# First step's values in place, dense weights in seven pieces, late values of two groups in whole tiles, own places for the first and last steps

## Chip, cores, metric

One core of a Trainium2 chip. The metric is the device time of one execution in microseconds (us), lower is better. The kernel before: median 1637.58 us of 3 runs (1636.99 to 1638.34). PE is TensorE, DVE VectorE, ACT ScalarE, POOL GpSimd, SP SyncE, whose queue issues most transfers.

## The reference

A recurrent attention layer (32 heads of 128, segments of 32 tokens, 8 memory rows carried from segment to segment) and a dense layer (512 to 1376 to 512), each applied twice to 2048 tokens:

```python
mem = mem0
for s in range(64):
    h = concat([mem, x[:, 32*s:32*s+32]])              # 40 rows
    q, k, v = h @ Wq, h @ Wk, h @ Wv                   # 32 heads
    o = softmax(mask(q @ k.T * scale)) @ v  @ Wo
    mem = o[:, :8]; outs.append(o[:, 8:])
# x += A(ln(x)); x += relu(ln(x) @ w1) @ w2; and both once more
```

Segment s+1 needs the memory rows of segment s: 64 steps in a row, four more because the second layer runs four steps behind the first.

## The kernel before

A planner written in Python holds every operation with a cost, an engine (or a choice of two) and a priority (`PLACE`, `AHEAD`: fitted numbers), simulates the engines, and emits the instructions in the order of the simulated starts. Each engine then works through its list strictly in that order. Cuts are marked `[...]`.

```python
# values of a step's own rows: product into vw, then small copies into V0
def step_values(k):
    [...]
    if 1 in act: values(...)                     # both layers
    else:        values_narrow(HTs[i][...])      # one layer: four strips
    place_values(k, False)                       # four DMAs V0 <- vw, step 0's on ACT's queue

# dense weights, once "loaded" holds (step 1's values are placed)
def load_dense():
    def dma1(): nc.sync.dma_start(out=w1_sb[:], in_=B_w1...)                 # 1376 KB
    def dma2(): nc.sync.dma_start(out=w2_sb[:, 0:NFC - 1, :], in_=B_w2...)   # 1280 KB
                [...]                                                         # and the rest, 96 rows

# values of the memory-independent rows of groups 6..15 ("late"), one group at a time,
# in tiles of 64 rows; layernorm two steps ahead of the first product
def late_values(g, xnT, ps, gate=()): [...]

o.prio = PERIOD * o.step + PLACE.get((o.key, o.step % 2), 0.0)   # same places for all steps
```

## Time and profile before

How to read it: the prediction below shows the page's busy shares, the table of stages, the starved stretch in step 1 and the loads of step 0. Of the rest of the page these two lines matter: how many packets the transfers make, and that one queue carries instructions.

```profile
DMA packets 35486, 64.30 MB, mean 39 GB/s; under 512 B 7224, under 2 KB 19232, under 8 KB 35104
q8 instruction: 318, 5.21, 1.3%
```

318 packets and 5.21 MB are 16 KB each: one block of 256 PE instructions per packet (PE and its weight loads have 81170 instructions, 317 blocks).

The stages used below are: step 0 (the weights stream in), steps 1, 2 and 3, the 60 wide steps (both layers at work), steps 64 to 66, and the last step with the tail. There is one trace of this kernel. Its execution took 1634.85 us, 2.7 us less than the median of the timed runs.

### The profile page before, as it was taken

Reading aid. Unit: us, or ns where it says so; the run is one execution under the profiler, and the core shown is the slowest. Engines: PE = TensorE matmul, PEld = TensorE weight load, DVE = VectorE, ACT = ScalarE, POOL = GpSimd, SP = SyncE. Lnnn points to the kernel's source line nnn. Section 1 sums busy time; section 2 is a strip of 40 time slices with the busy share of each in tenths; the row PEclk is TensorE's granted clock in tenths of the full one; section 3 lists DMA queues with packets and bytes.
Section 4 is the critical chain, followed back from the end, with each engine's and each line's share of the span. In section 5 each row is a group of like instructions: output and inputs, shape, how many; then the busy total and the mean of one; then the engine's idle time right before and its main releaser. Section 6 shows DMA issues by size and latency. Waiting matters only on the chain.

```text
span 1632.9 us, 89617 instructions
## 1 busy us (share of the span) xinstructions
PE 1592.1 (97%) x40555; PEld 1372.8 (84%) x40615; DVE 1124.5 (69%) x3113; ACT 1047.2 (64%) x2625; POOL 147.0 (9%) x354
## 2 busy tenths in 40 slices
PE   6899999999999999999999999999999999999998
PEld 4788888888888888888888888888888888888886
DVE  4476776776776676677677677667677766766765
ACT  4566666676666666666666666666666666666654
POOL 3110000010100000000000010010000000000010
PEclk9999999999999999999999999999999999999999
DMA  9711001110100110010010110011010000000000
GB/s 357 259 31 31 23 24 29 29 34 18 39 18 28 28 30 25 25 37 21 26 29 24 31 32 24 18 35 26 25 38 21 24 24 25 18 19 19 18 5 7
DMA packets 35486, 64.30 MB, mean 39 GB/s; under 512 B 7224, under 2 KB 19232, under 8 KB 35104
## 3 DMA queue, kind: packets, MB, share of 16 engines
q1 hardware_dynamic: 29216, 39.09, 8.6%
q0 software_dynamic: 4704, 18.35, 3.0%
q8 instruction: 318, 5.21, 1.3%
q10 hardware_dynamic: 1184, 1.12, 0.2%
q14 instruction: 64, 0.52, 0.1%
HBM read 33.50 MB, written 11.93 MB: 28 GB/s over the span
## 4 chain that ended last, share of the span: by engine, by line
PE 94%; DMA 2%; DVE 2%; ACT 1%; issue 1%; POOL 0%; POOLq 0%; DVEq 0%; ACTq 0%
PE work L907 37%; PE st L1046 19%; PE fill L827 16%; PE fill L527 10%; PE work L1019 4%; PE work L936 4%; PE work L527 2%; DMA Wk_sb<-in_A_Wk_dram 2%; ACT OT L763 1%; DVE HT L1062 0%; PE fill L636 0%; PE fill L846 0%; ACT PT L1000 0%; ACT es L958 0%; DMA V<-vw 0%
## 5 line engine op out<-in xcount | busy, mean ns | idle before, releaser
L907 PE MATMUL work<-HT,Wq_sb 128*128 128x80 bf16 (+1 forms) x8704 | 368.5, 200 | 8.4 <-DVE HT L1062 7.3
L907 PE MATMUL work<-HT,Wk_sb 128*128 128x80 bf16 (+1 forms) x8704 | 361.9, 200 | 3.7 <-DMA Wk_sb<-in_A_Wk_dram 2.5
L907 PEld LDWEIGHTS <-Wq_sb 128*128 128x128 bf16 x8704 | 325.7, 100 | 29.5 <-issue 14.8
L907 PEld LDWEIGHTS <-Wk_sb 128*128 128x128 bf16 x8704 | 326.3, 100 | 25.7 <-issue 13.6
L1046 PE MATMUL st<-OT,Wo_sb 128*128 128x80 bf16 (+1 forms) x8704 | 340.3, 200 | 3.3 <-issue 2.2
L1046 PEld LDWEIGHTS <-Wo_sb 128*128 128x128 bf16 x8704 | 320.2, 100 | 8.6 <-issue 4.9
L763 ACT CAST kT<-work 128x320 bf16<-128x320 f32 (+1 forms) x512 | 209.6, 409 | 99.1 <-PE work L907 59.2
L763 ACT CAST qT<-work 128x320 bf16<-128x320 f32 (+1 forms) x508 | 208.6, 411 | 89.9 <-PE work L907 43.9
L827 PE MATMUL fill<-Wv_sb,HT 128*64 128x512 bf16 x2048 | 259.1, 380 | 0.0
L1000 ACT ACTIVATE PT<-work,half 128x320 bf16<-128x320 f32 (+2 forms) x431 | 189.1, 466 | 56.2 <-PE work L527 35.5
L947 DVE TENSOR_TENSOR es<-work,maskb 128x320 f32<-128x320 f32 (+2 forms) x340 | 134.3, 403 | 111.6 <-PE work L936 93.9
L763 ACT CAST OT<-work 128x320 bf16<-128x320 f32 (+1 forms) x377 | 150.4, 415 | 63.5 <-PE work L1019 63.1
L763 ACT CAST vw<-fill 128x512 bf16<-128x512 f32 x204 | 119.4, 585 | 88.0 <-PE fill L827 80.1
L958 ACT ACTIVATE es<-es 128x320 f32<-128x320 f32 (+2 forms) x340 | 138.4, 409 | 42.8 <-DVE es L954 41.1
L954 DVE TENSOR_TENSOR es<-es,mx 128x320 f32<-128x320 f32 (+2 forms) x340 | 146.2, 439 | 4.5
L827 PEld LDWEIGHTS <-HT 128*64 128x64 bf16 x2048 | 98.5, 110 | 58.7
L951 DVE TENSOR_REDUCE mx<-es 128x8 f32<-128x320 f32 (+2 forms) x340 | 132.1, 398 | 4.4
L977 DVE TENSOR_TENSOR P<-es,sm 128x320 bf16<-128x320 f32 (+2 forms) x337 | 131.5, 406 | 3.4
L961 DVE TENSOR_REDUCE sm<-es 128x8 f32<-128x320 f32 (+2 forms) x340 | 131.3, 394 | 2.3 <-ACT es L958 2.0
L1002 DVE TENSOR_SCALAR PT<-work,half 128x320 bf16<-128x320 f32 (+2 forms) x249 | 109.3, 446 | 28.6 <-PE work L527 27.4
L936 PEld LDWEIGHTS <-qT 128*40 128x40 bf16 x4096 | 87.1, 98 | 44.3 <-issue 1.0
L1062 DVE CAST HT<-st 128x64 bf16<-128x64 f32 (+1 forms) x67 | 14.8, 221 | 157.8 <-PE st L1046 157.7
(91 smaller groups left out, 1807.9 us busy)
## 6 DMA issues: line engine op xcount, KB each, us to landing
V<-vw SPq DMA_DIRECT2D x252, 48.0 KB
V<-vh SPq DMA_DIRECT2D x120, 64.0 KB
vh<-vg SPq DMA_DIRECT2D x20, 256.0 KB
Wq_sb<-in_A_Wq_dram POOLq DMA_DIRECT2D x2, 2048.0 KB, 23.0
Wk_sb<-in_A_Wk_dram POOLq DMA_DIRECT2D x2, 2048.0 KB, 29.1
Wo_sb<-in_A_Wo_dram POOLq DMA_DIRECT2D x2, 2048.0 KB, 40.0
Wv_sb<-in_A_Wv_dram POOLq DMA_DIRECT2D x1, 2048.0 KB, 11.9
vh<-w_sb POOLq DMA_DIRECT2D x4, 512.0 KB, 10.6
```

Of the source, the lines that this page charges most:

```text
L527: nc.tensor.matmul(out_[u:v, :], lhsT=lhsT[:, u:v], rhs=rhs, start=start, stop=stop, tile_position=(0, u))
L763: nc.scalar.copy(out=out_, in_=in_)
L827: nc.tensor.matmul(vp[64 * b:64 * b + 64, :], lhsT=cols(c4), rhs=Wv_sb[:, c4, n * 512:(n + 1) * 512], start=(c4 == 0), stop=(c4 == NC4 - 1 ...
L907: nc.tensor.matmul(qp[:, hi * 2 * L:hi * 2 * L + n], lhsT=W_sb[:, c4, h * Dh:(h + 1) * Dh], rhs=HT[:, c4, c0:c1], start=(c4 == 0), stop=(c ...
L936: nc.tensor.matmul(v[64 * g2:64 * g2 + L, a, i, b, :], lhsT=qT[:, hi, a * L:(a + 1) * L], rhs=kT[:, hi, a * L:(a + 1) * L], start=True, st ...
L947: nc.vector.tensor_tensor(out=flat(es[:, A]), in0=flat(sp[:, A]), op=ALU.add, in1=maskb[:, a_lo:a_hi, :].unsqueeze(2).to_broadcast([128, n ...
L951: nc.vector.tensor_reduce(out=mx[:, As], in_=es3(), axis=AX.X, op=ALU.max)
L954: nc.vector.tensor_tensor(out=es3(), in0=es3(), op=ALU.subtract, in1=mx[:, As].unsqueeze(2).to_broadcast([128, ns * na, L]))
L958: nc.scalar.activation(out=es[:, A], in_=es[:, A], func=ACTF.Exp, scale=SCALE)
L977: (nc.gpsimd if eng == POOL else nc.vector).tensor_tensor(out=o, in0=flat(es[:, A]), op=ALU.mult, in1=sm[:, As].rearrange("p (a s) -> p a ...
L1000: nc.scalar.activation(out=o, in_=i, func=ACTF.Copy, scale=half[:, b:b + 1])
L1046: nc.tensor.matmul(wo[:, 2 * W * c4 + c0:2 * W * c4 + c1], lhsT=Wo_sb[:, h, c4 * 128:(c4 + 1) * 128], rhs=OT[:, h, c0:c1], start=(h == 0 a ...
```

## The change

Intent: a shorter step 0; no burst of dense weights that starves PE of instructions; fewer PE instructions for the late values; and priorities fitted for the first and last steps alone. The core of the diff (the tables of fitted numbers and the plumbing are cut):

```diff
-            o.prio = PERIOD * o.step + PLACE.get((o.key, o.step % 2), 0.0)
+            o.prio = PERIOD * o.step + PLACE.get((o.key, phase(o.step)), 0.0)
+def phase(step):
+    return 2 + (step > 0) + (step == 2) if step < DELTA else step % 2 + 5 * (step >= STEPS)
 [...]
+        if k == 0:
+            values_direct(HTs[0][:, :, 0:L], deps)      # products of 40 rows, evicted into V0
+            return
 [...]
-        for i, t, dma in ((0, 0.5, dma1), (1, 1.0, dma2)):
-            bulk(SP, t, dma, ("w", i), 1.4, r=["loaded", ...], w=[...])
+        def piece(at, fn, cost=0.5):                    # w1: 4 pieces, w2: 3
+            if at == (k, u):
+                bulk(SP, cost, fn, ("w", i), 0.35, r=["loaded", ("sc", k, u), ...], w=[("w", i)])
+        # at = (1,0) (1,1) (1,2) (1,3) | (1,4) (2,0) (2,1): scores of step k, unit u
 [...]
-    ahead, due = {}, {}                                 # one group at a time, first layernorm for step 4
+    start = {g: DELTA + 10 * i for i, g in enumerate(pairs)}    # pairs (6,7), (8,9), ...
+            if k == start[g] - 2:                       # first pair: layernorms in step 2
+                one = prepare_group(g, [("att", k - 1)])
+                late[g] = one, prepare_group(g + 1, [("att", k - 1)], one)
```

The lists `r=[...]` say what the planner places an operation behind.

## The prediction

> **What bounds the kernel now.** I read the page first: who is busy, and when.
>
> ```profile
> PE 1592.1 (97%) x40555; PEld 1372.8 (84%) x40615; DVE 1124.5 (69%) x3113; ACT 1047.2 (64%) x2625; POOL 147.0 (9%) x354
> ...
> PE   6899999999999999999999999999999999999998
> ...
> DMA  9711001110100110010010110011010000000000
> ```
>
> TensorE (PE) is full in every slice but the first two and the last; the DMA engines are full only in the first two slices (some 60 us, 40.8 us a slice) and nearly idle afterwards. So the end is set by PE, and what is not PE lies at the start and the end. The kernel is 68 dependent steps (a segment of 32 tokens each; two layers run four steps apart, so steps 0 to 3 and 64 to 67 hold one layer and the 60 between both). A step ends when VectorE copies the new memory rows (the evictions HT<-st, 67 of them). Cutting the trace at those gives: step 0, 1, 2, 3, the 60 wide steps, steps 64 to 66, the last with the tail.
>
> ```profile
> 0.00:55.08 55.08, 41.40 (x707) 26.38 (x707) 23.87 (x80) 26.39 (x59) 18.11 (x42) 0.97 0.99 359
> 55.08:73.92 18.84, 15.74 (x486) 13.78 (x486) 8.38 (x39) 9.87 (x35) 0.90 (x2) 0.93 0.72 251
> 73.92:92.83 18.91, 18.15 (x591) 15.73 (x591) 12.96 (x48) 10.76 (x38) 2.96 (x7) 0.98 0.21 52
> 92.83:108.70 15.87, 14.98 (x490) 13.14 (x490) 9.57 (x41) 10.20 (x36) 1.32 (x6) 1.00 0.13 29
> 108.70:1549.30 1440.60, 1427.35 (x36069) 1240.57 (x36127) 1021.70 (x2719) 945.33 (x2310) 118.26 (x286) 1.00 0.10 26
> 1549.30:1603.40 54.10, 52.96 (x1637) 45.14 (x1641) 35.11 (x139) 32.95 (x108) 4.22 (x10) 1.00 0.02 5
> 1603.40:1632.90 29.50, 21.49 (x577) 18.07 (x577) 12.94 (x49) 11.73 (x39) 1.24 (x3) 0.91 0.03 8
> ```
>
> (Columns: length, busy PE, weight loads, DVE, ACT, POOL, granted clock, DMA share, GB/s.) Of 40.8 us without PE, 13.7 are in step 0, 3.1 in step 1, 8.0 in the last window, and 13.3 in all 60 wide steps. The granted clock dips in step 1 and in the tail.
>
> The hole in step 1, in the timeline of PE:
>
> ```profile
> 68.16 0.74 PE L1046 MATMUL st<-OT,Wo_sb 128*128 128x40 bf16 x23
> 71.06 0.38 PE L1046 MATMUL st<-OT,Wo_sb 128*128 128x40 bf16 x9 [2.16 <-issue]
> 71.29 0.20 PE L527 MATMUL work<-ident,P 128*128 128x80 bf16 x1
> 71.32 0.29 PE L1019 MATMUL work<-PT,V 128*128 128x80 bf16 x2
> 71.41 1.27 PE L1046 MATMUL st<-OT,Wo_sb 128*128 128x40 bf16 x32
> ```
>
> A run of 32 projections stops after 23 and waits for no data ("issue"). Behind it 32 take 1.27 us where 0.97 is usual. In the records, full clock ends at 71.36 us and half clock lasts 3.41 us. Counting PE's instructions up to the hole and up to a smaller one (0.36 us at 76.1 us, also "issue"): 2241 and 2497, exactly 256 apart. The DMA queue marked "instruction" carries 16 KB packets, one per some 256 PE instructions; around the hole they start at 57.82, 61.33, then only 68.41 (ends 69.49, PE goes on 1.57 later), while the other queue moves 330 to 410 GB/s, mostly in 1 KB packets: the two dense weights, 1376 KB and 1280 KB in one transfer each, with five stores of activations. PE was starved of instructions by the dense loads.
>
> **What the skill says.** "Runtime: NRT & Kernel Launch", Instruction fetch mechanics: instructions are streamed in blocks of 16 KiB, 256 instructions, over DMA, normally hidden. The trace agrees on the size and shows one case where it was not hidden. "TensorE: Matmul & The Clock Gate", Part 1: idleness drops the PE clock to half, and the observing window is 3413 ns. The trace agrees: three half-clock stretches of 3.41 us, at 30.4, 71.4 and 1624.4 us, each after a gap of 2.5, 2.2 and 3.3 us. "DMA: Bandwidth & Descriptors", Queues, rings and completion order: each DMA engine takes turns between its queues packet by packet, so a bulk transfer delays others without owning them; the delayed fetch agrees. "TensorEngine Tiling (Array Packing)", Key Properties: changing the tiling mode drains TensorE; here it costs 97 ns from start to start (80-column matmul to scores 131 against 36).
>
> **The change, part by part.** I compared both instruction orders. The matmul streams are the same but for 623 fewer instructions (40615 to 39992), mostly pairs of half-width tiles becoming whole tiles. A pair of half tiles runs concurrently, so that is no PE time by itself.
>
> *Late values of two groups in whole tiles.* Before: 10 groups x 32 matmuls of 64 rows, two at a time: 320/2 x 216 ns = 34.6 us. After: 5 pairs x 32 matmuls of 128 rows: 160 x 216 = 34.6 us. Nothing gained. Mode changes: 375 before, 377 after, +0.2 us. Their stores go from 20 of 256 KB to 40 of 128 KB on a queue that has time. One buffer holds the pair, so five of the layernorm transposes that filled a step boundary move inside a step: bare boundaries (last projection straight to next Q or K) go from 27 to 31. Each boundary costs 520 ns against 36, and a transpose filled 0.22 of it: about +0.6 us.
>
> *First step in place.* Before, step 0's values took 32 matmuls in four strips (1.7 us), went to a buffer, and six DMAs on ScalarE's queue placed them (four of 48 KB, two of 64 KB). After: 32 in two strips (3.5 us), evicted straight to their place. PE work +1.7 us, but step 0 is bound by the weight stream: the last Wo half lands at 53.2 us (issue 11.0 + 42.2) and its 64 projections start at 53.27.
>
> ```profile
> Wo_sb<-in_A_Wo_dram POOLq DMA_DIRECT2D x2, 2048.0 KB, 40.0
> ...
> V<-vw ACTq DMA_DIRECT2D x4, 48.0 KB
> ```
>
> The six small DMAs ran from 17.8 to 30 us; there the rate falls from 405 to 254 GB/s, and Wk's first half comes late:
>
> ```profile
> 25.82 1.90 PE L827 MATMUL fill<-Wv_sb,xg 128*64 128x512 bf16 x16
> 30.18 1.01 PE L907 MATMUL work<-HT,Wk_sb 128*128 128x40 bf16 x27 [2.47 <-DMA Wk_sb<-in_A_Wk_dram]
> ```
>
> Without them 0.32 MB less is moved (0.8 us at 400 GB/s), and the engines that lagged stay level; I take 2 us off the last weight's landing, so step 0 ends at 53.1 instead of 55.08. The 2.5 us gap and its half clock mostly vanish, but inside a step bound elsewhere: not counted twice. **-2.0 us.**
>
> *Dense weights in seven pieces.* Each of 256 to 512 KB, released by the scores of successive units of steps 1 and 2, so the queue is never full for 4 us on end. Gone: 2.16 + 0.36 us of starvation and half of 3.41 us of half clock (1.7). **-4.2 us**, on PE's path.
>
> *Own places for first and last steps.* Only the planner's priorities. For the 60 wide steps, adding up start-to-start times (80 columns 35.9 ns, 40 columns 25.2, 128 columns 55.7, 512 columns 216 per tile set, 97 per mode change, 520 at a boundary) gives 1413.8 us before and 1412.8 after: the same. The measured 1440.6 leaves 27; the same sum misses some 0.26 us in steps where I see no wait, so true waits are about 11 us. They sit in odd steps: 22.08 us without a late-values operation, 22.48 with one, 23.02 with two (0.87 us of work each), so part of each fills a hole. After has 5, 10 and 15 such steps, before 4, 12 and 14: no difference to speak of. From better places I take **-1.5 us** here, and **-0.7** in steps 64 to 67 (65 measures 18.9 against a sum of 17.0); the final chain (turn, layernorm, dense, store) has the same operations.
>
> Sum: -2.0 - 4.2 + 0.8 - 1.5 - 0.7 = -7.6: 1637.58 to 1630.0 us.
>
> **Rivals.** (1) *The hole moves instead of vanishing*: the activations' stores (five of 128 KB, 1 KB packets) and the first pair's load still share steps 1 and 2 with the pieces, and 40-column steps use up 256 instructions in some 3.2 us, so another fetch may be late. For it: a block must arrive within about 0.75 of a block. Against: the 18 MB of weights and stores through the software queue before 59 us stopped no fetch. Time: 1634. (2) *Step 0 gains nothing*: after Wk's second half the new order has 11.5 us of PE work, before 10.5; if PE rather than Wo is last, 1632. (3) *New transfers hurt*: the late groups' activation stores become 1024 pieces of 128 bytes each, on the queue that also places values each step; a late placement would stall attention ten times by a microsecond: +5 to 10. Against: placements have over 10 us from their source to their use. (4) *Steady state improves much*: if the search removed the whole 11 us: 1621.
>
> **Range and chances.** The parts I can point at are worth 6 us; the places lie between -11 and +4. Range 1623 to 1637. Over 2% faster means below 1605, 33 us: more than all of step 0's and the tail's waits together, 0.02. Slower by 2% would need a new wait of half a microsecond in each step: 0.01. Within 2%: 0.97.
>
> **What would show it.** Right: no "issue" gap over 1 us between 55 and 95 us and full clock there; step 1 near 15.5 us; first memory eviction near 53; no DMA to V on ScalarE's queue; wide steps summing to 1436 to 1442; the tail still 29 us. Wrong: a starved gap elsewhere, first eviction at 55 or later, or two-step periods other than 47.4 to 48.4 us.

## The result, and the profile after

| | median | range | runs |
|---|---|---|---|
| before | 1637.28 us | 1636.60 to 1638.34 | 4 |
| changed | 1636.09 us | 1633.76 to 1636.44 | 4 |

Ratio 0.9989, 95% interval 0.9972 to 1.0006: the same. (Ratios are the mean time of one kernel's fast runs over that of the other's of the same rounds, so not quite the ratio of the medians.) The 7.6 us that I forecast are not there; later the changed kernel came out at ratios of 1.0002 and 1.0002. Its 15 runs have a mean of 1636.13 us, the 44 runs of the kernel before 1635.82.

The page after (busy PE, packets, the instruction queue):

```profile
PE 1589.6 (97%) x39898; PEld 1377.3 (84%) x39992; DVE 1111.6 (68%) x3091; ACT 1052.5 (64%) x2655; POOL 140.1 (9%) x352
DMA packets 47097, 63.89 MB, mean 39 GB/s; under 512 B 17784, under 2 KB 33440, under 8 KB 46720
q8 instruction: 313, 5.13, 1.4%
```

Instructions fell as intended (five blocks fewer), packets under 512 B went up by 10560, mostly the stores of late activations (ten of 1024 pieces). The table of stages, cut at the same evictions as before (length, busy PE, weight loads, DVE, ACT, POOL, clock, DMA share, GB/s):

```profile
0.00:52.65 52.65, 41.39 (x713) 26.81 (x713) 25.39 (x82) 28.10 (x61) 18.49 (x43) 1.00 0.98 369
52.65:70.62 17.97, 16.37 (x486) 13.55 (x486) 9.05 (x41) 9.96 (x35) 0.90 (x2) 0.91 0.61 206
70.62:89.86 19.24, 17.98 (x597) 15.92 (x599) 12.51 (x49) 11.56 (x40) 4.09 (x9) 1.00 0.43 116
89.86:106.84 16.98, 16.35 (x497) 13.48 (x497) 11.56 (x43) 11.37 (x39) 1.61 (x5) 1.00 0.25 48
106.84:1548.71 1441.87, 1423.17 (x35411) 1243.70 (x35503) 1005.50 (x2691) 945.56 (x2330) 111.10 (x283) 1.00 0.11 26
1548.71:1602.28 53.57, 52.85 (x1616) 45.50 (x1619) 34.84 (x138) 33.91 (x111) 3.12 (x8) 1.00 0.02 5
1602.28:1632.00 29.72, 21.45 (x582) 18.32 (x582) 12.72 (x49) 12.06 (x40) 0.79 (x2) 0.91 0.03 7
```

Step 0 is 2.43 us shorter, as forecast. Steps 1 and 2 should have given 4.2 us and gave 0.5; step 3 is 1.1 longer, and the wide steps 1.3. In step 2, PE stops again for nothing that is named (timeline of PE: start, length, what; in brackets the idle time before it):

```profile
83.56 0.19 PE L1214 MATMUL st<-OT,Wo_sb 128*128 128x40 bf16 x1
84.55 0.95 PE L1214 MATMUL st<-OT,Wo_sb 128*128 128x40 bf16 x31 [0.80 <-issue]
```

It stops after one projection of 32. This profiled run was the fastest of the four (1633.76). A second profile, of the same program, shows the same place at its worse, and what it does to step 2 (its line of the stage table; the clock is the seventh entry, 0.85):

```profile
83.94 0.19 PE L1214 MATMUL st<-OT,Wo_sb 128*128 128x40 bf16 x1
87.25 1.21 PE L1214 MATMUL st<-OT,Wo_sb 128*128 128x40 bf16 x31 [3.12 <-issue]
...
70.86:94.37 23.51, 19.84 (x597) 17.51 (x599) 12.52 (x50) 11.57 (x40) 4.09 (x9) 0.85 0.35 95
```

Counting PE's instructions from the start, the hole stands at 12.75 blocks of 256. The holes of the kernel before stood at 8.75 and 9.75 (2241 and 2497 instructions). In the second profile the packet with the next block starts at 84.8 us, when PE has already stopped; the blocks around it start their packets when PE is at 11.14 and 13.14. So the starvation was not removed. It moved to another boundary.

Why are the pieces not spread? The queue of SP (when it was busy with which issue):

```profile
62.24 1.81 SPq L514 DMA_DIRECT2D w_sb<-in_B_w_dram  x4
...
64.58 1.39 SPq L803 DMA_DIRECT2D xe<-in_A_x_dram  x1
...
66.49 1.39 SPq L811 DMA_DIRECT2D xh<-xg  x3
```

All four pieces of w1 go out in 1.81 us. In the plan each stands behind its unit's scores *and* behind "loaded" (the values of step 1 placed). But these are marks of the planner: they fix the place in SP's list, and the emitting loop then only calls the operations in that order. In none of the 18 traces does a transfer `w_sb<-in_B_w_dram` wait for a semaphore that PE raises; nearly all wait for earlier transfers alone, a few for VectorE as well. So no score releases a piece at run time. The four stand side by side in the list, behind the four copies into V, whose issues end at 61.6 us, and go out one after the other. The queue then moves 311 to 388 GB/s from 64 to 69 us. The last two w2 pieces go out together at 79.4 us, with 1024 packets of 128 bytes ahead of them, and move 341 and 329 GB/s from 82 to 84, just when block 12 is due (82.1 to 84.8 in the two profiles).

The table shows a second thing. `xe` is the input of the first late group. It stands behind the four pieces, and VectorE needs it (timeline of DVE, then of PE):

```profile
69.79 0.69 DVE L684 BATCH_NORM_STATS2 ln<-xe 128x6 f32<-128x512 bf16 x1 [1.14 <-DMA xe<-in_A_x_dram]
...
70.62 0.16 DVE L1230 CAST HT<-st 128x32 bf16<-128x32 f32 x1
```

```profile
70.83 0.34 PE L1074 MATMUL work<-HT,Wk_sb 128*128 128x40 bf16 x7 [0.84 <-DVE HT L1230]
```

The line after `xe` is the copy of the new memory rows, which starts the next step. VectorE keeps its order, so the late layernorm's wait for a transfer becomes PE's wait between steps 1 and 2. In the kernel before, the first such layernorm was at 107 us, after the dense weights.

### The profile page after: what moved, and what is told of

It reads as the page before. It is cut to its first block, busy times and chain, and to the rows that moved or that the text cites. A ratio compares the mean times of both kernels' runs of the same rounds, so it can differ in the third digit from the quotient of the medians.

```text
span 1632.0 us, 88442 instructions
## 1 busy us (share of the span) xinstructions
PE 1589.6 (97%) x39898; PEld 1377.3 (84%) x39992; DVE 1111.6 (68%) x3091; ACT 1052.5 (64%) x2655; POOL 140.1 (9%) x352
## 4 chain that ended last, share of the span: by engine, by line
PE 92%; DMA 3%; DVE 2%; ACT 2%; issue 1%; POOL 0%; ACTq 0%; SPq 0%; POOLq 0%; DVEq 0%
PE work L1074 37%; PE st L1214 18%; PE fill L973 14%; PE fill L646 10%; PE work L1187 4%; PE work L1103 4%; DMA Wo_sb<-in_A_Wo_dram 2%; PE work L646 2%; PE fill L944 2%; ACT OT L894 1%; DVE HT L1230 0%; PE fill L992 0%; DMA vw<-in_A_x_dram 0%; ACT es L1125 0%; ACT PT L1168 0%
## 5 line engine op out<-in xcount | busy, mean ns | idle before, releaser
L1074 PE MATMUL work<-HT,Wk_sb 128*128 128x80 bf16 (+1 forms) x8704 | 355.7, 199 | 9.6 <-DVE HT L1230 8.8
L1074 PE MATMUL work<-HT,Wq_sb 128*128 128x80 bf16 (+1 forms) x8704 | 349.3, 199 | 1.3 <-DVE HT L1230 0.9
L1214 PEld LDWEIGHTS <-Wo_sb 128*128 128x128 bf16 x8704 | 324.9, 99 | 28.0 <-issue 5.2
L1074 PEld LDWEIGHTS <-Wq_sb 128*128 128x128 bf16 x8704 | 320.4, 99 | 26.4 <-issue 15.1
L894 ACT CAST qT<-work 128x320 bf16<-128x320 f32 (+1 forms) x534 | 219.5, 412 | 76.8 <-PE work L1074 32.4
L973 PE MATMUL fill<-Wv_sb,HT 128*64 128x512 bf16 x2048 | 265.9, 381 | 0.0
L894 ACT CAST OT<-work 128x320 bf16<-128x320 f32 (+1 forms) x404 | 158.1, 417 | 119.8 <-PE work L1187 117.3
L1168 ACT ACTIVATE PT<-work,half 128x320 bf16<-128x320 f32 (+2 forms) x384 | 170.9, 468 | 67.1 <-PE work L646 47.0
L1114 DVE TENSOR_TENSOR es<-work,maskb 128x320 f32<-128x320 f32 (+2 forms) x340 | 136.8, 404 | 45.2 <-PE work L1103 40.3
L1170 DVE TENSOR_SCALAR PT<-work,half 128x160 bf16<-128x160 f32 (+2 forms) x296 | 127.5, 454 | 25.1 <-PE work L646 23.4
L1121 DVE TENSOR_TENSOR es<-es,mx 128x320 f32<-128x320 f32 (+2 forms) x340 | 136.7, 405 | 5.5
L1103 PEld LDWEIGHTS <-qT 128*40 128x40 bf16 x4096 | 90.8, 98 | 44.8 <-ACT kT L894 10.2
```

What stands on the lines that cost most here:

```text
L894: nc.scalar.copy(out=out_, in_=in_)
L973: nc.tensor.matmul(vp[64 * b:64 * b + 64, :], lhsT=cols(c4), rhs=Wv_sb[:, c4, n * 512:(n + 1) * 512], start=(c4 == 0), stop=(c4 == NC4 - 1 ...
L1074: nc.tensor.matmul(qp[:, hi * 2 * L:hi * 2 * L + n], lhsT=W_sb[:, c4, h * Dh:(h + 1) * Dh], rhs=HT[:, c4, c0:c1], start=(c4 == 0), stop=(c ...
L1103: nc.tensor.matmul(v[64 * g2:64 * g2 + L, a, i, b, :], lhsT=qT[:, hi, a * L:(a + 1) * L], rhs=kT[:, hi, a * L:(a + 1) * L], start=True, st ...
L1114: nc.vector.tensor_tensor(out=flat(es[:, A]), in0=flat(sp[:, A]), op=ALU.add, in1=maskb[:, a_lo:a_hi, :].unsqueeze(2).to_broadcast([128, n ...
L1121: nc.vector.tensor_tensor(out=es3(), in0=es3(), op=ALU.subtract, in1=mx[:, As].unsqueeze(2).to_broadcast([128, ns * na, L]))
```

## The experiments

All outputs are right. The kernel before ran in the same rounds; its medians were 1636.68 (first four runs), 1635.44 (next four), 1635.61 and 1635.61. The times alone settle little: executions of one and the same kernel spread over 5 us. So I split steps 1 and 2, where the kernels differ most, into three parts for every trace: holes over 0.3 us at a count of n.75 blocks ("boundary"), half of PE's busy time in half-clock stretches ("half clock", an estimate), and the rest. Each row has one trace; e6, e12, e13 and e17 are in the text alone.

| kernel | median us (range) | ratio (95%) | step 0 | steps 1+2 | boundary | half clock | rest |
|---|---|---|---|---|---|---|---|
| before | | | 55.08 | 37.75 | 2.5 | 1.6 | 33.7 |
| changed, first profile | 1636.09 | 0.9989 | 52.65 | 37.21 | 0.8 | 1.7 | 34.7 |
| e1 changed again | 1636.66 (1635.94-1638.35) | 1.0002 (0.9990-1.0015) | 52.16 | 42.20 | 4.4 | 4.6 | 33.1 |
| e16 changed again | 1635.19 (1633.28-1638.65) | 1.0002 (0.9990-1.0013) | 52.31 | 40.26 | 2.6 | 3.4 | 34.2 |
| e2 before + pieces | 1636.40 (1636.16-1636.73) | 0.9998 (0.9986-1.0011) | 55.83 | 38.54 | 2.4 | 3.1 | 33.1 |
| e3 changed, whole loads | 1636.61 (1635.59-1637.77) | 1.0000 (0.9987-1.0012) | 52.09 | 41.39 | 2.1 | 3.4 | 35.9 |
| e4 idle products | 1635.96 (1633.45-1636.76) | 0.9992 (0.9979-1.0006) | 53.43 | 41.06 | 2.0 | 2.9 | 36.2 |
| e5 stores later | 1635.17 (1631.73-1637.19) | 0.9997 (0.9985-1.0009) | 52.37 | 39.95 | 3.7 | 1.7 | 34.6 |
| e8 pieces spread | 1634.36 (1633.61-1635.57) | 0.9995 (0.9983-1.0006) | 52.46 | 39.04 | 2.5 | 1.7 | 34.9 |
| e10 values by copy | 1640.36 (1636.77-1643.31) | 1.0031 (1.0019-1.0043) | 58.13 | 37.94 | 0.5 | 1.7 | 35.7 |
| e11 input early | 1634.19 (1633.31-1638.74) | 0.9999 (0.9987-1.0012) | 52.94 | 39.33 | 2.9 | 3.0 | 33.4 |
| e14 e11 + spread | 1634.72 (1632.93-1637.59) | 0.9997 (0.9985-1.0010) | 53.89 | 40.07 | 3.5 | 1.7 | 34.8 |
| e15 all early | 1637.06 (1633.84-1638.39) | 1.0010 (0.9998-1.0023) | 53.13 | 36.61 | 1.1 | 0.0 | 35.5 |
| e18 changed + 128 instr. | 1640.12 (1638.38-1642.58) | 1.0031 (1.0019-1.0043) | 55.84 | 41.40 | 4.1 | 4.7 | 32.7 |

### Is the result what it seems? (e1, e16)

No edit: the changed kernel again.

> The changed kernel once more, unaltered, for a second profile and a tighter interval. Theory A (the windows in which the PE clock is granted run free of the kernel): steps without a clock change repeat to 0.1 us (wide steps 1441.9 us in all), while the half-clock stretch at 53.2 us may fall elsewhere or be absent, so steps 0 to 3 may differ from 106.84 us by up to 1.7 us either way. Theory B (the stretch is tied to the wait for Wo): it stands again within 0.5 us of 53.2. Time against the kernel before: 0.9985 to 0.9995, so -0.8 to -2.5 us.

> The changed kernel again, unedited, beside the candidates on the same chip. Expected 1635.5 to 1636.7; its profile shows again holes at boundaries n.75 of 256 instructions of between 2 and 5 us in steps 1 and 2 together, and the sum of steps 0 to 3 somewhere between 106.8 and 111.3 us.

Ratios 1.0002 both. Steps 1 and 2 took 42.2 and 40.3 us, so the first profile (37.2) was a lucky one. The wide steps took 1441.87, 1440.91 and 1440.73 us: they repeat to about 1 us, not to the 0.1 us that I expected. Theory B is refuted: the half clock of 53.2 us stands at 55.6 in e1, and e16 has none before 73.1. Half clock explains part of the spread: of the 15 executions, the one with a mean granted clock of 0.998 took 1633.28 us, five with 0.997 averaged 1635.50, six with 0.996 1636.51, three with 0.995 1637.39. A thousandth of 1634 us is 3.3 us at half clock, about one window of 3.41 us; one more such window costs some 1.2 us (an estimate: a straight line through the 15, which leaves more than half of their variance unexplained).

### The pieces alone, and the rest without them (e2, e3)

```diff
 # e2: the kernel before, with
-            load_dense()                      # two whole transfers
+            load_dense(k, u)                  # seven pieces, as in the change
 # e3: the changed kernel, with
-            load_dense(k, u)
+            load_dense()                      # two whole transfers in step 1
```

> The kernel before with the dense weights in seven pieces and nothing else: the orders of PE, ACT and DVE are identical, only 14 lines of the DMA queue's order differ. Theory A (the hole at 68.9 us is instruction starvation by the two large loads): the 2.16 us and 0.36 us holes and the half clock at 71.4 us go, step 1 falls from 18.84 to about 15.5 and step 2 from 18.91 to about 18.2, the whole by 4 us (1633.2). Rival (the stores of the activations starve it as well): a hole of 0.5 to 1.5 us stays somewhere in steps 1 to 2, gain 1 to 2.5 us. Rival 2 (the hole has another cause): same hole, no gain.

> The changed kernel with the dense weights loaded in two transfers as before; PE, ACT and DVE orders identical. Theory A: a hole of about 2 us marked issue comes back in step 1 or 2, about two thirds into an instruction block, with a half-clock stretch after it: +3 to +4 us against the changed kernel (1639 to 1640). Rival (the new order of the first steps alone avoids the starvation, the pieces are worth nothing): within 0.5 us of the changed kernel.

The instruction orders of PE, ACT and DVE are those of the parent kernel in both, so only transfers differ. With pieces, the kernel before loses its hole at 8.75 and gets one of 2.05 us at 12.76; boundary losses are 2.4 us against 2.5. Without pieces, the changed kernel has 0.54 us at 8.76, 0.40 at 12.75 and 1.14 at 5.75. Times: the same. The pieces move the starvation; they are worth nothing measurable.

### Keeping the clock up (e4)

```diff
+                for _ in range(22 if k == 0 and p == 2 else 0):     # while PE waits for Wo
+                    nc.tensor.matmul(wo[:, 384:512], lhsT=ident, rhs=ident, start=False, stop=False)
```

> The changed kernel with 22 idle matmuls (ident by ident, 128 columns, 55.7 ns each, 1.2 us) into unused columns of the projection bank while PE waits for the last Wo half. Theory A (that wait[...] halves the clock from 53.2 to 56.6 us): no half clock between 12 and 1620 us, step 0 unchanged at 52.6 +- 0.3, step 1 17.97 to about 16.3, whole -1.7 us. Rival (the half clock comes from the steps' low use of the array in general): a stretch appears in another window of steps 1 to 3, gain below 0.5 us.

The half-clock stretch at 53 us is gone, but so it is in e11, e14, e15 and e16 without such products: that they removed it is not shown. PE did not wait for Wo in this execution, so the products came on top, and step 0 ends at 53.43 us, not at 52.6 as expected. A stretch of 6.8 us comes at 72.9, after a wait for the late input, here at its longest (DVE, then PE):

```profile
72.94 0.69 DVE L685 BATCH_NORM_STATS2 ln<-xe 128x6 f32<-128x512 bf16 x1 [4.03 <-DMA xe<-in_A_x_dram]
...
73.77 0.16 DVE L1234 CAST HT<-st 128x32 bf16<-128x32 f32 x1
```

```profile
73.99 0.71 PE L1075 MATMUL work<-HT,Wk_sb 128*128 128x40 bf16 x16 [3.73 <-DVE HT L1234]
```

This trace is what made the second cause plain: PE waits 3.73 us for a copy that takes 0.16 us and whose engine stood waiting for `xe`.

### Which transfer starves block 12? (e5, e8, e15)

```diff
 # e5: the late pair's 128-byte stores from step 2 to step 5
+            elif g <= EARLY + 2: held.append(put_op)
 # e8: e5, and each piece is planned behind a different later operation of PE
+GATE = (scores 1.2, attention 1.0, projection 1.2, projection 1.4,
+        queries/keys 2.0, scores 2.1, scores 2.2)
 # e15: e8, input of the late pair loaded in step 0, and the last pieces earlier
+GATE = (scores 1.2, attention 1.0, projection 1.1, projection 1.2,
+        projection 1.4, queries/keys 2.0, queries/keys 2.0)
```

> The changed kernel with one thing moved: the two stores of the first late pair's activations (1024 pieces of 128 bytes each) go from step 2 to step 5; only four lines of the SyncE order differ. Theory A, the small stores delay the fetch of the instruction block that ends in step 2: no hole of 0.4 to 3.1 us at the boundary 12.75 in the trace, step 2 is 18.0 to 18.8 us (19.2 to 23.5 in the runs so far), and the median falls to about 1635. Theory B, the weight pieces beside them do it (or a fetch slow by itself): the hole stays, step 2 is 19 us or longer, the median is 1636 to 1637.

> As the run before, and the seven dense pieces are really spread: each waits for a later piece of TensorE work (scores of step 1, attention of step 1, two output projections of step 1, queries and keys of step 2, scores of step 2 twice), so that no two pieces are issued together. The orders on PE, ACT and POOL are unchanged. Theory A, starvation comes of a queue that is full for 4 us: from 64 to 86 us no 4 us have over 250 GB/s, PE has no hole over 0.4 us at a block boundary from 55 us on, steps 1 to 3 sum to 51.5 to 52.5 us (54.2 in the trace of the changed kernel, 56 to 59 in later ones), and the median is 1633 to 1634.5. Theory B, the fetch is late for another reason (any transfer, or the fetches of the other engines): holes of 0.5 us or more stay, steps 1 to 3 sum to 54 us or more, the median is 1636 to 1637.

> Candidate to beat both: the orders of PE, ACT and POOL as in the changed kernel, first late input loaded in step 0, the 128-byte stores in step 5, and all seven dense pieces issued before step 2's value placements (the last two some 6 us earlier than in the run before), so that nothing large moves when instruction block 12 is to be fetched. Theory, the hole at 12.75 is the backlog of the last two pieces: it falls to 0.5 us or less (0.4 with whole early transfers, 1.2 to 3.1 where pieces were issued at 79 to 82 us); steps 1 and 2 take 34 to 36 us; median 1632 to 1634. Rival, the short instructions of the dense layer outrun the fetch whatever moves: the hole stays at 1 us or more, median 1634.5 to 1636.

e5 refutes the small stores: they are gone and the hole at 12.75 is 2.58 us. e8 was my mistake in part: its last pieces still went out together (SP's queue; then PE's hole at 12.75):

```profile
79.56 1.35 SPq L520 DMA_DIRECT2D w_sb<-in_B_w_dram  x2
80.96 0.45 SPq L522 DMA_DIRECT2D w_sb<-in_B_w_dram  x1
```

```profile
86.34 0.82 PE L1215 MATMUL st<-OT,Wo_sb 128*128 128x40 bf16 x26 [1.22 <-issue]
```

The four copies into V0 of step 2 keep SP's queue busy from 76.0 to 79.5, and what was to be spread piled up behind them. (VectorE's order is not quite that of the changed kernel in e8, e14 and e15; those of PE, ACT and POOL are.) In e15 all pieces are issued by 73.1 us. Then the hole at 12.75 is gone (block 12's packet starts when PE is at 11.90), and there is one at 10.76, where the pieces now move:

```profile
76.05 0.25 PE L1104 MATMUL work<-kT,qT 128*40 128x40 bf16 x6
77.37 0.30 PE L1104 MATMUL work<-kT,qT 128*40 128x40 bf16 x10 [1.07 <-issue]
```

So the backlog of weights makes the large hole, and it falls on the block that is due while they move. This rests on single traces, but the difference is clear: in the twelve traces in which the last two pieces are issued together, 78 to 87 us from the start, with the places and the counts of the two kernels, the hole at 12.75 is 0.5 to 3.1 us. Steps 1 and 2 took 36.61 us without any half clock, the best of all traces. But that profile was the fastest of five executions (1633.84 us), and the median is 1637.06: no gain. What the slower four did is not in a trace.

### Is it instruction fetch? (e18, e17)

```diff
+                for _ in range(64 if k == 0 and heads[0] == 8 and W_sb is Wq_sb else 0):
+                    nc.tensor.matmul(qp[:, 384:388], lhsT=ident, rhs=ident[:, 0:4], start=False, stop=False)
```

128 more instructions in step 0, nothing else (e18); the same on top of e15 (e17).

> The changed kernel with the same 64 idle products in step 0 and nothing else. Theory, instruction fetch: the holes keep standing at a count of n.75 blocks of 256 instructions, now counted with the 128 added ones, so in front of other products than before (not ahead of the third output projection of step 2). Rival, the hole is a wait of that projection for something that the profile does not name: it stays with the projection, at a count of n.25.

> The first run of this call with 64 idle products of 4 columns added to TensorE in step 0 (128 instructions with their weight loads), which moves every block boundary by half a block in the program. If the short instructions of the dense layer make the hole of block 12, the boundary now lies 128 instructions earlier in the work and the hole changes by half a us or more; if the backlog alone makes it, nothing changes but the 0 to 1.5 us that the products cost in step 0. Median 1632.5 to 1635.

In e18 the holes stand at 9.76 and 13.75 blocks, counted with the added instructions. In the changed kernel PE stopped after the first of a unit's 32 products. In e18 that product has the count 13.25; PE passes it without a stop and stops 128 instructions later, ahead of the last product of the next unit (the second pair of lines; the first pair is the other hole, in step 1):

```profile
71.50 0.51 PE L1218 MATMUL st<-OT,Wo_sb 128*128 128x40 bf16 x14
74.39 0.61 PE L1218 MATMUL st<-OT,Wo_sb 128*128 128x40 bf16 x18 [2.38 <-issue]
...
89.81 0.94 PE L1218 MATMUL st<-OT,Wo_sb 128*128 128x40 bf16 x31
92.42 0.19 PE L1218 MATMUL st<-OT,Wo_sb 128*128 128x40 bf16 x1 [1.68 <-issue]
```

A wait for data would have stayed with its product. It is the count that decides. Step 0 is 3.5 us longer in e18, not 0 to 1.5 (55.84 us; 56.56 in e17). Of this 1.9 us are two holes at 4.75 and 5.75 blocks (0.53 and 1.35 us), which now fall into step 0 and are late fetches again; the rest is the time of the products. So e18's 1640.12 us and e17's 1638.66 (1635.84 to 1639.52, ratio 1.0015, 1.0003 to 1.0027) are mostly that price. In e17 the holes of steps 1 and 2 are small (0.71 us at 12.76, 0.41 at 13.76), but the first ends at 86.6 us, and from 82 us on the DMA moves 60 GB/s or less. In e3 there are 0.40 us at 12.75, at 88 us, though its weights had moved by 79. So small holes come without a backlog at that moment; whether the short instructions outrun the fetch there, the rival of e15, stays open.

### The late input (e11, e14, e12, e13)

```diff
 # e11: the first late input is loaded one step earlier, its layernorm stays where it was
-                one = prepare_group(g, [("att", k - 1)])
+                one = prepare_group(g, [("att", k - 1 - (k == 2))])
 # e14: e11, e5 and spread pieces
 # e12: all late pairs two steps later;  e13: e12 and spread pieces
-    start = {g: DELTA + 10 * i ...}
+    start = {g: DELTA + 2 + 10 * i ...}
```

> The changed kernel with the load of the first late pair's input issued in step 0 rather than in step 1 behind the dense pieces; the orders of PE, ACT, DVE and POOL are those of the changed kernel. Theory, a new wait made by the change: the first late layernorm now stands in VectorE's order before the memory columns of step 2, and its input lands behind the dense weights. Then VectorE's wait for that input (0.6 to 4.0 us in the five traces so far) is gone before the columns of step 2, TensorE waits under 0.4 us between steps 1 and 2 (0.8 to 3.7), and the median falls by 0.5 to 1.5 us against the changed kernel of the same call's level, to 1634.5 to 1636. Rival, the wait only shows where something else is late: TensorE still waits 0.8 us or more there for another cause, median as before.

> The candidate to beat both kernels: early load of the first late input, dense pieces spread (as in the run before), the 128-byte stores of the first late pair in step 5. PE, ACT and POOL order as in the changed kernel. By the three causes found: steps 1 and 2 without boundary holes after step 0 and without the wait for the late input take 34.5 to 36 us (37.2 to 42.2 in the changed kernel), of it 1.2 us the hole of block 5.75 that the weights make; median 1632.5 to 1634. If half-clock stretches fall there whatever is done, 1.7 us more: 1634.5 to 1635.5.

> The changed kernel with all late pairs two steps later (first late layernorms in step 4, where no dense weights move). Orders change in many steps. Same theory: no wait for the late input between steps 1 and 2, steps 0 to 3 sum to 107 to 109 us; but the planned order has steps 2, 4 and 5 longer by 2.1, 0.6 and 0.3 us than that of the changed kernel and steps 3 and 6 on shorter by 0.9 and some more, so the median is 1635 to 1637. If the wide steps lose their fitted order as they did without own places: 1640 or more.

> The run before with the seven dense pieces spread, the last two now by queries and keys and by attention of step 2. Theory, holes at instruction-block boundaries come of a full queue: the hole at boundary 12.75 (1.2 us in the first spread kernel, 0.4 to 3.1 elsewhere) is under 0.5 us; steps 0 to 3 are 1 to 2 us shorter than in the run before; median 1634 to 1635. Rival, spread or not is the same: within 0.5 us of the run before.

In e11 the orders of PE, ACT, DVE and POOL are untouched, and VectorE now comes to the copy early and waits for PE:

```profile
67.79 0.68 DVE L684 BATCH_NORM_STATS2 ln<-xe 128x6 f32<-128x512 bf16 x1
...
69.25 0.19 DVE L1230 CAST HT<-st 128x32 bf16<-128x32 f32 x1 [0.56 <-PE st L1214]
```

PE waits under 0.3 us there. Step 1 takes 16.31 us (17.97, 18.70 and 18.24 in the changed kernel), but the half clock or the hole at 5.75 that those traces have in step 1 were absent too, so this is not the wait's worth alone. That the wait was real and that the change made it is shown. But the hole at 12.75 took 2.87 us, a half-clock stretch of 6.8 us followed, and the median is 1634.19, ratio 0.9999: one cause of three removed does not show in the time. e14 removes this one and parts of the others: 0.9997. It had both a late fetch at 5.75 (1.65 us) and at 12.75 (1.33), since in step 2 SP was again busy with the copies until 80.4 us. e12 and e13 take the layernorm out of step 2 as well, but the planner then finds a worse order: step 2 takes 23.6 and 23.2 us, the wide steps 1442.8 and 1443.3; medians 1639.58 (1.0031, 1.0018 to 1.0045) and 1639.11 (1.0021, 1.0009 to 1.0034).

### Values in place, and own places (e10, e6)

```diff
 # e10: step 0's values through the side buffer and six DMAs again, early inputs in two buffers of their own
-            values_direct(HTs[0][:, :, 0:L], deps)
-            return
+            pass
 # e6: the places of the wide steps for all steps
-    return 2 + (step > 0) + (step == 2) if step < DELTA else step % 2 + 5 * (step >= STEPS)
+    return step % 2
 # and the numbers of the other engines (part(), which goes with AHEAD) likewise
-    return 1 if step < DELTA else 2 * (step >= STEPS)
+    return 0
```

> The changed kernel with step 0's values as before: two narrow products into the side buffer, then copies by DMA into the rows of the value tile, early activations in two tiles of their own again. If the predicted step 0 gain of 2.0 us is real and is kept to the end: step 0 ends at 54.6 us or later (52.1 to 52.7 with direct values) and the median is 1638 to 1639. If step 0 gains but a later hole takes it back: step 0 as said, the sum of steps 0 to 3 within 1 us of the changed kernel's 110, and the median 1636 to 1637. If the gain came of the earlier weights alone and not of the values: step 0 ends at about 53.

> The changed kernel with the own places undone: all steps take the places fitted for the wide steps, so the order of steps 0 to 3 and 64 to 67 changes, and no instruction is added or taken away. If own places are worth what I predicted for the end (0.7 us) and something at the start: steps 64 to 66 sum to 54.3 us or more (53.6 with own places, 54.1 before), steps 0 to 3 are 1 us or more longer, median 1638 or more. If they are worth nothing: 1636 to 1637.

e10: step 0 is 5.8 us longer than in the changed kernel (mean 52.37), the time 4 to 5 us. More than the 2.7 us between the two kernels, since the priorities were fitted with the direct values; it is an upper bound. In its trace PE waits 2.7 us for the copies into V (1.80 and 0.91), and 10.2 us of half clock fall on it from 47.0 us on. It also shows a giving back: without the earlier step 0, the hole at block 5.75 (1.0 to 1.7 us in e1, e3, e4, e5, e8, e12, e13, e14 and e16) is absent, and boundary losses are 0.5 us.

e6: 1662.68 us (1661.72 to 1664.88), ratio 1.0169 (1.0155 to 1.0182), 26 us more than the changed kernel, far beyond what I expected either way. Step 0 takes 58.8 us, steps 64 to 66 60.4, and even the wide steps, whose own numbers are unedited, 1454.1. The planner's wide steps grow out of the state in which the first steps leave the engines. Since the kernel before does as well with one set for all steps, this says that the numbers are fitted as one set, not that own places are worth 27 us. What own places alone are worth stays open.

No version beat both kernels: the lowest ratios of the experiments are e4's 0.9992 and e8's 0.9995, and the intervals of both include 1.

## Why the prediction was wrong

Means of the three profiles of the changed kernel against the one of before (1634.85 us, 1.0 under the mean of the timed ones), so the last column is about 1 us too hard on the change in sum:

| step of the prediction | predicted | in the traces |
|---|---|---|
| step 0 in place | -2.0 | -2.7 (55.08 to 52.37) |
| dense pieces: steps 1 and 2 | -4.2 | +2.1 (37.75 to 39.90) |
| late values, boundaries, wide places: step 3 and the wide steps | +0.8 - 1.5 | +1.7 (1456.47 to 1458.16) |
| steps 64 to 67 | -0.7 | +0.2 (83.60 to 83.82) |
| sum | -7.6 | +1.3; timed runs: +0.3 (1636.13 against 1635.82) |

**Dense pieces: the step that failed.** "Released by the scores of successive units of steps 1 and 2, so the queue is never full for 4 us on end": wrong. I read marks of the plan as waits of the program. No piece waits for a score; four stand side by side in SP's list and go out within 1.81 us, and the last two go out together because SP's queue is busy before. Boundary losses in steps 1 and 2 averaged 2.6 us in the three profiles, 2.5 before: of the 2.52 us that I wrote off as starvation, nothing went. Half clock there costs 3.3 us (estimate) where it cost 1.6: why, is not shown. The remaining 0.3 includes the late input, below. This is the first rival, "the hole moves instead of vanishing", to which I gave 1634; I dismissed it because the weights and stores had stopped no fetch before 59 us. That holds for the kernel before only: with the shorter step 0, PE reaches the boundary 5.75 at 53.1 us (e1) and stands there for 1.0 to 1.7 us in most traces. What moves then, at 410 GB/s, is no longer a weight (the last landed at 50.3) but the stores of the early values (`vh<-w_sb`, the last landed at 56.8). So about a half of the gain in step 0 is given back right after it.

**A wait that I did not list.** I noted the first late pair's load as traffic in steps 1 and 2, but not that VectorE's order puts its layernorm ahead of the memory rows. It cost PE 0.84 and 1.06 us in two of the three profiles (under 0.3 in the third), 1.8 in e3 and 3.7 in e4; with the input loaded early (e11) it is gone. The comparison of orders, which I had, showed both instructions.

**Step 0: right in its cause and nearly in size, only in part in its path.** Without the six copies the rate is 401 and 411 GB/s from 24 to 27 and from 27 to 30 us (331 and 264 before), the last half of Wo lands at 50.8, 50.3 and 50.2 us (53.2 before), and no copy to V is on ACT's queue. But that step 0 was "bound by the weight stream" is half of it. Before, PE worked without a pause from 30.2 to 52.5 us and then waited for ACT until 53.16, when Wo happened to land (53.18). In e2, with the same orders, it waited for ACT in the same way, though Wo had landed at 52.91 (PE of the kernel before, then of e2):

```profile
53.20 0.23 PE L1019 MATMUL work<-PT,V 128*128 128x80 bf16 x2 [0.68 <-ACT PT L1000]
...
53.95 0.23 PE L1031 MATMUL work<-PT,V 128*128 128x80 bf16 x2 [0.68 <-ACT PT L1012]
54.02 1.77 PE L1058 MATMUL st<-OT,Wo_sb 128*128 128x40 bf16 x64
```

So two limits stood together: the landing of Wo, and PE's own work behind the 2.47 us wait for Wk and its half clock. I set that wait aside as "inside a step bound elsewhere"; had it stayed, the earlier Wo would have gained little. It went as well, by the same cause, so that the sum came out has some luck in it. In e1 and e16 PE no longer waits for Wo, as the second rival has it.

**Late values: right that whole tiles gain nothing**, odd wide steps take 22.09, 22.47 and 23.01 us with none, one and two such operations (22.08, 22.48, 23.02 before). The mis-sized term is places in the wide steps, -1.5: they gave nothing. Step 3 is 1.1 us longer since late products now fall into it, and five pairs' layernorms may be what makes a few even wide steps 0.1 to 0.6 us longer (25.5 to 26.0 us against 25.4).

**The end:** steps 64 to 66 gained 0.5 us; the last step's chain is unchanged and its half clock lasts 3.4 or 6.8 us as the window falls (29.7, 30.7 and 30.3 us), which eats it.

The range 1623 to 1637 and the chance of 0.97 for "within 2%" held, the range by its width; the centre was 6 us too low.

## What to carry to other kernels

When a transfer is split and gated, ask first whether the gate is a wait in the program or only a place in a plan. Where it is a place, pieces that stand side by side go out together, and a queue that is busy before gathers more of them. Before work is moved earlier on an in-order engine, look at what stands behind it there and whether its input can be late. And a difference of 1 us in 1636 can't be read from one profile when single executions spread over 5: split the stage into its causes, count each in several traces, and repeat the unedited kernel.

## What the Trainium skill lacked or had wrong

- "Runtime: NRT & Kernel Launch", Instruction fetch mechanics, calls block crossings "mostly hidden" and gives PE 2048 instructions of room, but speaks of two lines of 16 KB as well. Here PE stopped for 0.3 to 3.1 us at crossings, always at 0.75 of a block, when the packet of the next block started late (in e1 with PE at 12.75 rather than at about 12.1); PE went on about 1.5 us after the packet's end. That speaks for the small number: with eight blocks ahead, a fetch late by 3 us would not be seen. The page lacks what makes it visible: 256 instructions of 40-column products with their weight loads last only 3.2 us (25.2 ns for a pair), and, at the larger holes, another queue was moving over 300 GB/s.
- "TensorE: Matmul & The Clock Gate", Part 1, has as a rule no idle gaps over about 3.4 us. Here shorter gaps in stretches of 40-column products, from 1.2 us (for Wo, first profile of the changed kernel) to 3.1 us (e1), were followed by half clock of 3.41 or 6.83 us, while one of 2.58 us (e5) was not. How much of a window must be idle stays open. The page's free-running window agrees: in every trace the half-clock stretches start whole multiples of 3.41 us apart (12 and 455 windows in the kernel before), and the first one stands at 53.2, 55.6 and 73.1 us in the three profiles of the changed kernel. By the mean granted clock (0.998 to 0.995), that kernel spent some 2 to 5 windows at half clock from one execution to the next (an estimate).
- No page that I read says by how much a lone packet of one queue is delayed behind another queue that is full: the instruction packets started up to 0.65 of a block, some 2 us, later than in stretches without bulk traffic.
